# Attention beside a state-space scan on one core: two-bank ScalarE groups with an optional third bank, shared with VectorE

## The chip, the cores and the metric

The kernel runs on one core of one Trainium2 chip. The metric is the time of one execution in microseconds (us), as the device measures it. The program uses TensorE (PE), ScalarE (ACT), VectorE (DVE) and GpSimd (POOL), which work at the same time (busy for 93, 97, 87 and 57% of one span of 767.2 us in before) and which it makes wait for each other by semaphores, and a DMA queue (SP). Its matmuls write into PSUM, which it uses as eight banks of 128 x 512 fp32 numbers.

A run more than 1.5% above the fastest of its kernel counts as slow and is left out. A ratio below is the mean time of one kernel's fast runs over that of the other's fast runs of the same rounds, so it is not quite the ratio of the medians beside it. Brackets after a ratio are its 95% interval.

## The reference

Two independent layers, written side by side into one output.

```python
def _A_ref(x, Lambda_re, Lambda_im, B_re, B_im, C_re, C_im, log_dt, Dskip):   # x: 1 x 2048 x 640
    Lam_bar = jnp.exp(dt * Lam)                      # a complex diagonal state-space model
    Bu = jnp.einsum("bld,pd->blp", x + 0j, B_bar)
    for t in range(L):
        h = Lam_bar[None, :] * h + Bu[:, t, :]       # ... the scan over time
    return 2.0 * jnp.einsum("blp,dp->bld", hseq, Cmat).real + x * Dskip

def _B_ref(x, wq, wk, wv, wo):                       # 32 query heads of 20, one key and value head
    scores = jnp.einsum("bhqd,bkd->bhqk", q, k) * (Dh ** -0.5)
    p = _softmax(scores, axis=-1)                    # 32 x 2048 x 2048 exponentials
    o = jnp.einsum("bhqk,bkd->bhqd", p, v)
    return o.reshape(...) @ wo
# output: concatenate([a, b], axis=-1), bf16
```

The exponentials are what costs time. They are cut into 2048 tiles of 128 keys x 512 queries.

## The kernel before

The Python program is a planner. It keeps a list of operations with estimated durations, plays them through a simple model of the engines, and emits for each engine the order that the model chose. The order is fixed when the kernel is built.

A score tile goes one of two ways. *ScalarE tiles* are scored into a slot of several banks, and one ScalarE instruction exponentiates the whole slot into bf16 tiles "PR". *VectorE tiles* ("D" in the code) are scored into one bank, and VectorE makes an approximate exponential from integer arithmetic: one eviction "DR<-MB", then three shifted copies "DR<-DR", which VectorE or GpSimd make. The value matmuls then read PR or DR. PE, ScalarE and VectorE thus share 2048 tiles, and every tile that VectorE takes is one less for ScalarE.

```python
class Build:
    CHUNKS = (3, 2)     # two ScalarE slots: one of three banks, one of two
    MISC = 2            # two banks for VectorE score tiles and all other tasks; one more collects values
    NPS = 8             # eight exp buffers of three tiles each
    NDS = 18            # exp buffers of VectorE tiles
    SHARE = 0.25        # at most this share of tiles for VectorE
...
    def fill(self, op, i):                      # refill ScalarE slot i
        t, banks = self.slots[i]
        n = min(self.CHUNKS[i], NTILE - self.tile_n)
        h = self.hold[self.nhold % self.NPS]
        self.nhold += 1
        extra, used = [], set()
        while len(extra) < 4 - n and self.want_d(len(extra)):   # VectorE tiles scored beside it
            m = self.take_d(used)
            ...
            extra.append(m)
        tiles = [self.take_tile(used) for _ in range(n)]
        ...                                     # n score matmuls, then the extra ones
        dst = p.PR[:, h.index, 0:n, :]
        ex = self.act(lambda e: e.activation(dst, t[:, 0:512 * n], ACT.Exp, scale=1.0 / UNIT), ...)
...
    def want_d(self, taken=0):                  # may VectorE have another tile now?
        ...
        if len(self.d_banks()) <= taken:        # needs a free bank
            return False
        return len(self.d_free()) > taken + len(self.SHIFTS) - 1   # and free DR buffers
```

The state-space layer runs in the background as "tasks" in the misc banks: input matmuls (`xaT,BT` in the trace), a chain of VectorE rotations and scans, output matmuls (`CT`). PE also issues *filler* matmuls (`KT,VZ`) when the planner sees too little PE work in the last 3 us.

Of the kernel before, what the change touches and what calls it, by code (L numbers as in the profile page):

```python
# [9 lines left out]
ALU = mybir.AluOpType  # L10
AX = mybir.AxisListType
FP32 = mybir.dt.float32
BF16 = mybir.dt.bfloat16
# [26 lines left out]
class Schedule:  # L40
# [10 lines left out]
    SWITCH, STAY = 97.0, 1.2  # L51


    PAUSE = 1000.0
    LOCK = 60.0
    TABLE = 1280.0

# [329 lines left out]
class Holder:  # L387


    def __init__(self, index):  # L390
        self.index = index
        self.left = 0
        self.users = []
        self.taken = False
        self.waits = False


S, D, NC, H, DH = 2048, 640, 5, 32, 20
NQB, NKC, NGG = 4, 16, 8
# [5 lines left out]


class Build:
    CHUNKS = (3, 2)
    MISC = 2
    NPS = 8  # L410
    NOP = 7
    NRD = 3
    NDS = 18
# [16 lines left out]
    def build(self):  # L430
        nc = self.nc
        with ExitStack() as o:
            self.banks = []
            self.slots = []
            nb = 0
            for i, n in enumerate(self.CHUNKS):
                t = o.enter_context(nc.psum_tensor(f"SC{i}", [128, 512 * n], FP32))
                bs = [Bank(t, 512 * k, f"B{nb + k}") for k in range(n)]
                nb += n
                self.banks += bs  # L440
                self.slots.append((t, bs))
            rest = []
            for i in range(8 - nb):
                t = o.enter_context(nc.psum_tensor(f"MB{i}", [128, 512], FP32))
                rest.append(Bank(t, 0, f"B{nb + i}"))
            self.banks += rest
            self.pvbank = rest[-1]
            self.misc = rest[:self.MISC]
            self.early = [b for b in self.banks if b not in rest]
            self.alloc(o)  # L450
            base = nc.sbuf_bytes_remaining
            with ExitStack() as p1:
                self.alloc_early(p1)
                early = base - nc.sbuf_bytes_remaining
            with ExitStack() as p2:
                self.alloc_late(p2)
                late = base - nc.sbuf_bytes_remaining
                if late < early:
                    self.sb(p2, "pad", [128, (early - late) // 4 + 8], FP32)
                self.program()  # L460
                self.s.run()
                shares = {k: self.EARLY for k in self.LATE}
                shares.update({f"W{c}_1": [f"xbT{i}_{k}" for i in range(2) for k in range(NC)] for c in range(NC)})
                shares.update({f"CT{tb}_{c}": [f"xn{tb}"] for tb in range(2) for c in range(NC)})
                em = Emitter(nc, self.s.order, [b.key for b in self.banks], shares)
                em.plan()
                with nc.Block() as block:
                    em.emit(block)

    def alloc(self, o):  # L470
# [13 lines left out]
        self.VZ = sb(o, "VZ", [128, 32], BF16)  # L484
        self.WO = sb(o, "WO", [128, NC, 640], BF16)
        self.WOt = sb(o, "WOt", [128, 640], BF16)
        self.PR = sb(o, "PR", [128, self.NPS, max(self.CHUNKS), 512], BF16)
        self.tab = sb(o, "tab", [128, 2, NC, 512], BF16)
        self.Z = sb(o, "Z", [128, 2, NC, 512], BF16)
        self.prod = sb(o, "prod", [128, 4, 2, 512], BF16)  # L490
# [112 lines left out]
    def program(self):  # L603
# [7 lines left out]
        self.q_op, self.qd_op, self.half_op, self.scat_op, self.rd_op, self.brow_op = {}, {}, {}, {}, {}, {}  # L611
        self.o_ops, self.y_ops, self.w_op, self.xa_op = {}, {}, {}, {}
        self.state_op = {}
        self.hold = [Holder(i) for i in range(self.NPS)]
        self.nhold = 0
        self.dhold = [Holder(i) for i in range(self.NDS)]
        self.d_open = []
        self.d_left = collections.defaultdict(int)
# [24 lines left out]
    def warm_source(self):  # L643

        if self.started or self.s.t > 40000.0:
            return None
        p = self
        return Op("pe", [self.mm(self.pvbank.ap, p.PR[:, 0, 0, 0:128], p.PR[:, 0, 0, :], True, True)], 260.0, prio=9,
                  load=512.0, deps=[self.zero_op], reads=["PR0"], writes=[self.pvbank.key], hook=self.warm_last)


# [22 lines left out]
        self.pvbank.last = [op]  # L674

    def constants(self):
        self.zero_op = self.dve(lambda e: e.memset(self.PR[:, 0, 0, :], 0.0), 200, writes=["PR0"], prio=0.1)
        p = self
        self.c_op = {}

# [192 lines left out]
        self.give(bank)  # L873

    def take(self, which=None):
        for b in self.free_banks:
            if which is None or b in which:
                self.free_banks.remove(b)
                b.busy = True
                return b  # L880
        raise RuntimeError("no bank")
# [35 lines left out]
    def qt_task(self, bank):  # L917

        p = self
        prev = self.pe(self.four(bank, [p.VZ[:]] * 4, p.PR[:, 0, 0, :], True, False), self.mmt(512),  # L920
                       deps=[self.c_op["VZ"], self.zero_op] + bank.last, prio=0.95, mode="C", reads=["VZ", "PR0"], writes=[bank.key])
        for c in range(NC):
            prev = self.pe(self.four(bank, [p.wqf[:, 640 * c + 20 * j:640 * c + 20 * j + 20] for j in range(4)], p.xbT[:, c, 0:512],
# [108 lines left out]
    def attention(self):  # L1032
# [7 lines left out]
        fill = None  # L1040
        self.slot_last = [[op for b in bs for op in b.last] for _, bs in self.slots]
        self.pv_gate = list(self.pvbank.last)
        while self.tile_n < NTILE:
            i = k % len(self.slots)
            yield lambda: (fill is None or fill.start is not None) and all(o.start is not None
# [17 lines left out]

        for i in (k % 2, (k + 1) % 2):
            yield lambda: fill.start is not None and all(o.start is not None for o in self.slot_last[i])
            for bank in self.slots[i][1]:
                bank.last, bank.busy = list(self.slot_last[i]), False
                self.misc.append(bank)
                self.free_banks.append(bank)

    MARGIN = 650.0

# [21 lines left out]
    def fill(self, op, i):  # L1094
        p = self
        t, banks = self.slots[i]
        n = min(self.CHUNKS[i], NTILE - self.tile_n)
        h = self.hold[self.nhold % self.NPS]
        self.nhold += 1
        extra, used = [], set()  # L1100
        while len(extra) < 4 - n and self.want_d(len(extra)):
            m = self.take_d(used)
            if m is None:
                break
            extra.append(m)
        tiles = [self.take_tile(used) for _ in range(n)]
        ents = []
        for x, m in enumerate(tiles):
            b, kc, j = self.score(op, m, t[:, 512 * x:512 * x + 512], banks[x])
            ents.append((b, kc, j, p.PR[:, h.index, x, :]))  # L1110
        for m in extra:
            self.fill_d(op, m)
        op.reads = sorted(set(op.reads))
        op.dur = self.mmt(512, len(op.fns))
        op.load = 128.0 * len(op.fns)
        dst = p.PR[:, h.index, 0:n, :]
        ex = self.act(lambda e: e.activation(dst, t[:, 0:512 * n], ACT.Exp, scale=1.0 / UNIT),  # L1117
                      0.8333 * 512 * n + 64, table="exp",
                      deps=[op], reads=[b.key for b in banks[:n]], writes=[f"PR{h.index}"], prio=0.5,
                      gate=lambda: not h.taken or (h.left == 0 and self.s.done(h.users)))  # L1120

        def on_start(_):
            h.taken, h.left, h.users, h.waits = True, n, [], False
        h.waits = True
        ex.hook = on_start
        self.slot_last[i] = [ex]
        for b, kc, j, rhs in ents:
            self.pvq[b][j].append((p.VP[:, kc, 0:32], kc, rhs, f"PR{h.index}", ex, h, "VP"))
            self.pv_filled[b] += 1

    def score(self, op, m, out, bank):

# [65 lines left out]
    def want_d(self, taken=0):  # L1198
        s = self.s
        if self.tile_n >= NTILE - 8 or self.d_count + taken + 1 > self.SHARE * (self.tile_n - 16):  # L1200
            return False
        if len(self.d_banks()) <= taken:
            return False
        return len(self.d_free()) > taken + len(self.SHIFTS) - 1

# [27 lines left out]
        bank.last = [op]  # L1233
        self.give(bank)

    def fill_d(self, op, m):

        p = self
        bank = self.d_banks()[0]
        self.take([bank])  # L1240
        h = self.d_free()[0]
        self.d_count += 1
# [93 lines left out]
    def pv_source(self):  # L1336
# [16 lines left out]
            return None  # L1353
        complete = self.pv_filled[b] == 64 and not any(self.d_left[b, j] for j in range(4))
        left = sum(len(x) for x in q)
        h = self.hold[self.nhold % self.NPS]
        tight = h.taken and h.left > 0 or any(x.waits and x.left > 0 for x in self.hold)
        if len(group) < 4 and not tight and not (complete and left < 12 and len(group) == sum(1 for x in q if x)):
            return None
        prio = 0.9 if tight else self.PV  # L1360
        return Op("pe", [], self.mmt(512, len(group)), prio=prio, mode="C", load=128.0 * len(group), hook=lambda op: self.pv(op, b, group))

    def vp_seen(self, kc, t):
# [164 lines left out]
    def finish(self, prev, rows, bank, ops, end=None):  # L1528
# [3 lines left out]
        if end is None:  # L1532
            i = self.outs % 4
            self.outs += 1
            key, st = f"stg{i}", self.stg[:, i, :]
        else:
            key, st = f"PR{end}", self.PR[:, end, 0, :]
        last = self.stage_dma.get(key)
        if end in (4, 1, 3):
            ev = self.act(lambda e: e.activation(st, bank.ap, ACT.Copy), 600, deps=[prev], reads=[bank.key], writes=[key], prio=1)  # L1540
# [11 lines left out]
    def ssm_scalars(self):  # L1552
# [126 lines left out]
                               deps=self.ct_op[1], reads=[f"CT1_{c}" for c in range(NC)], writes=[f"CT1_{c}" for c in range(NC)], prio=3)  # L1679

        for c in range(NC):
            self.diag_op = self.dve(self.ts(p.diagD[:, c, :], p.ident[:], sc[:, DSK, c:c + 1], None, ALU.mult), 160,
                                    deps=[sc_op, self.c_op["ident"]], reads=["sc", "ident"], writes=["diagD"], prio=3)

    def unit_task(self, tb, c, ri, bank):
# [269 lines left out]
```

## Time and profile before

The median was 768.67 us (768.52 to 770.01, four runs).

| read from the profile of before | value |
|---|---|
| span of the profiled run | 767.2 us |
| ScalarE tiles / groups | 1604 / 642 |
| VectorE tiles | 444 |
| exponentials, merged busy time (overlaps counted once) | 726.7 us |
| idle of ScalarE just before exponentials | 5.7 us |
| first exponential starts / last one ends | 23.46 / 755.61 us |
| tail after the last exponential | 11.6 us |

From the page of before: the busy time of each engine, its share of the span and its instructions.

```profile
span 767.2 us, 24010 instructions
PE 716.6 (93%) x10217; PEld 239.1 (31%) x10217; DVE 666.2 (87%) x1239; ACT 743.2 (97%) x668; POOL 435.8 (57%) x454
```

The groups of instructions of before, each shape apart. The columns are line, engine, operation, output<-input, shapes, count, busy us and mean ns of one, then the idle time of the engine just before them and what ended it.

```profile
L1117 ACT ACTIVATE PR<-SC 128x1536 bf16<-128x1536 f32 x321 | 510.0, 1589 | 4.2 <-PE MB L585 2.5 <-PE SC L585 1.5
L600 DVE TENSOR_SCALAR DR<-MB 128x512 int16<-128x512 f32 x444 | 295.7, 684 | 64.2 <-PE MB L585 59.0 <-POOL DR L595 0.2
L1117 ACT ACTIVATE PR<-SC 128x1024 bf16<-128x1024 f32 x320 | 372.7, 1165 | 1.5 <-PE MB L585 1.4
```

The idle column is the one to read first. ScalarE never waits: 4.2 + 1.5 us before 641 exponentials. VectorE waits 64 us before its evictions, for PE to score something into a bank. So ScalarE is the limit, and VectorE has room but gets its tiles too late or too few. The mean durations (1589 and 1165 ns) overlap their neighbours, so their sum exceeds the time that they fill (510.0 + 372.7 us against 726.7 merged). The cost of a group has to be read from a stretch without gaps, as in this line of the windows of before for the tile PR (the second number under ACT is the count of exponentials):

```profile
core 0: us, PE busy (x) PEld busy (x) DVE busy (x) ACT busy (x), PEclk, DMA share, GB/s
510.00:657.00 147.00, 45.35 (x317) 11.58 (x317) 0.00 (x0) 147.00 (x131) 1.00 0.07 18
```

131 groups of 2.5 tiles on average in 147.0 us are 1.122 us each.

The timeline of ScalarE in before, merged; a bracket is idle time before the piece and what ended it. Gaps above a microsecond are rare.

```profile
23.46 4.62 ACT L1117 ACTIVATE PR<-SC 128x1536 bf16<-128x1536 f32 x4 [0.23 <-PE SC L585]
29.18 302.51 ACT L1117 ACTIVATE PR<-SC 128x1536 bf16<-128x1536 f32 x267 [1.10 <-PE SC L585]
333.06 68.82 ACT L1117 ACTIVATE PR<-SC 128x1024 bf16<-128x1024 f32 x61 [1.38 <-PE MB L585]
699.38 56.23 ACT L1117 ACTIVATE PR<-SC 128x1536 bf16<-128x1536 f32 x50 [1.91 <-PE MB L585]
```

### The profile page before, as it was taken

To read this page: it belongs to the slowest core of one execution; us is meant where nothing else is said; L and a number is where in the kernel's file an instruction comes from. 1 tells how busy PE (TensorE), PEld (TensorE's weight loads), DVE (VectorE), ACT (ScalarE), POOL (GpSimd) and SP (SyncE) were. 2 spreads that over 40 slices of the span, in tenths; PEclk is the share of its full clock that TensorE was granted. 3 is DMA by queue.
4 is the path that set the end of the run, shared out by engine and by line. 5 is a ranking of instruction groups with operands and counts; after the bars stand their busy time and mean duration, and the time that the engine had idled before them with its cause. 6 is when DMAs were issued, how large, how long until landed. Compare 5 with 4: busy or idle time off the path is not lost.

```text
span 767.2 us, 24010 instructions
## 1 busy us (share of the span) xinstructions
PE 716.6 (93%) x10217; PEld 239.1 (31%) x10217; DVE 666.2 (87%) x1239; ACT 743.2 (97%) x668; POOL 435.8 (57%) x454
## 2 busy tenths in 40 slices
PE   9999999998999999999889999999989999999997
PEld 3332223232223243332233322323322332233223
DVE  6989999898999888989899888998988889984786
ACT  5999999999999999999999999999999999999994
POOL 4765666466556544467635565446556556556961
PEclk9999999999999999999999999999999999999999
DMA  9934200100001111020001111120000110001001
GB/s 189 139 92 99 67 18 10 47 12 10 9 16 25 35 31 56 25 48 14 7 12 35 32 31 35 46 50 17 11 18 14 25 25 22 16 11 28 25 10 42
DMA packets 61770, 27.87 MB, mean 36 GB/s; under 512 B 44936, under 2 KB 61664, under 8 KB 61664
## 3 DMA queue, kind: packets, MB, share of 16 engines
q1 hardware_dynamic: 60332, 26.20, 14.7%
q8 instruction: 81, 1.33, 0.7%
q10 hardware_dynamic: 1332, 0.13, 0.2%
q14 instruction: 25, 0.20, 0.1%
HBM read 8.31 MB, written 8.12 MB: 21 GB/s over the span
## 4 chain that ended last, share of the span: by engine, by line
ACT 81%; PE 13%; DVE 3%; DMA 1%; SPq 1%; issue 0%; POOL 0%; ACTq 0%; DVEq 0%; POOLq 0%
ACT PR L1117 81%; PE MB L581 5%; PE MB L585 4%; PE SC L585 4%; DMA wqf<-in_B_wq_dram 1%; PE SC L581 1%; SPq L570 0%; DMA xaT<-in_A_x_dram 0%; DVE diagD L599 0%; DVE QP L956 0%; POOL fr L600 0%; DVE rot L1651 0%; DVE mab L814 0%; DVE prod L599 0%; DVE fr L600 0%
## 5 line engine op out<-in xcount | busy, mean ns | idle before, releaser
L1117 ACT ACTIVATE PR<-SC 128x1536 bf16<-128x1536 f32 (+1 forms) x642 | 726.7, 1376 | 5.7 <-PE MB L585 3.8
L595 POOL TENSOR_TENSOR DR<-DR,step 128x512 int32<-128x512 int32 x406 | 414.9, 1046 | 300.5 <-DVE DR L600 146.1
L600 DVE TENSOR_SCALAR DR<-MB 128x512 int16<-128x512 f32 x444 | 295.7, 684 | 64.2 <-PE MB L585 59.0
L585 PE MATMUL SC<-QT,KT 32*128 32x512 bf16 x1604 | 250.6, 385 | 40.0 <-ACT PR L1117 30.2
L585 PE MATMUL MB<-DR,VS 128*32 128x512 bf16 x1776 | 233.4, 385 | 0.4 <-DVE pvsb L1385 0.2
L585 PE MATMUL MB<-PR,VP 128*32 128x512 bf16 x1604 | 220.3, 385 | 0.9 <-DVE pvsb L1385 0.6
L585 PE MATMUL MB<-QT,KT 32*128 32x512 bf16 x444 | 160.4, 384 | 0.4 <-DVE prod L595 0.3
L585 PEld LDWEIGHTS SC<-QT,KT 32*128 32x128 bf16 x1604 | 63.9, 91 | 265.4 <-ACT PR L1117 179.8
L600 DVE TENSOR_SCALAR DR<-DR 128x1024 int16<-128x1024 int16 (+1 forms) x290 | 102.8, 408 | 7.9 <-PE MB L585 6.7
L585 PEld LDWEIGHTS MB<-DR,VS 128*32 128x32 bf16 x1776 | 59.5, 94 | 66.0 <-issue 38.1
L585 PEld LDWEIGHTS MB<-PR,VP 128*32 128x32 bf16 x1604 | 55.9, 94 | 63.2 <-issue 42.9
L581 PE MATMUL MB<-xaT,BT 128*32 128x512 bf16 x800 | 59.3, 383 | 0.4 <-DMA xaT<-in_A_x_dram 0.2
L595 DVE TENSOR_TENSOR prod<-MB,Z 128x1024 bf16<-128x1024 f32 x40 | 48.6, 1215 | 4.9 <-PE MB L581 4.4
L585 PE MATMUL MB<-KT,VZ 128*32 128x256 bf16 x876 | 48.5, 275 | 0.0
L585 PEld LDWEIGHTS MB<-QT,KT 32*128 32x128 bf16 x444 | 38.1, 91 | 24.1 <-issue 14.8
L1725 DVE TENSOR_TENSOR_SCAN g<-sc,hst,u 128x512 bf16<-128x512 f32 x30 | 39.6, 1327 | 0.0
L595 DVE TENSOR_TENSOR prod<-g,tab 128x1024 bf16<-128x1024 bf16 x40 | 31.4, 786 | 0.0
L581 PE MATMUL MB<-xbT,wqf 128*32 128x512 bf16 x400 | 29.6, 391 | 0.5 <-DVE DR L600 0.2
L581 PE MATMUL MB<-CT,W 128*32 128x512 bf16 (+1 forms) x640 | 29.4, 301 | 0.2 <-DVE DR L600 0.2
L581 PE MATMUL MB<-CT,xbT 128*32 128x512 bf16 (+1 forms) x640 | 28.5, 301 | 0.6 <-issue 0.4
L1542 DVE CAST stg<-MB 128x512 bf16<-128x512 f32 x35 | 24.0, 685 | 5.6 <-PE MB L581 5.3
L581 PE MATMUL MB<-WO,OP 128*32 128x128 bf16 (+1 forms) x580 | 27.1, 293 | 0.2
(137 smaller groups left out, 363.8 us busy)
## 6 DMA issues: line engine op xcount, KB each, us to landing
out_dram<-stg SPq DMA_DIRECT2D x35, 128.0 KB, 1.7
qd<-QP SPq DMA_DIRECT2D x20, 128.0 KB, 1.7
QT<-qd SPq DMA_DIRECT2D x28, 80.0 KB
OP<-pvsb SPq DMA_DIRECT2D x108, 20.0 KB
rdP<-recs SPq DMA_DIRECT2D x108, 20.0 KB
CT<-in_B_x_dram SPq DMA_DIRECT2D x2, 640.0 KB, 5.8
WO<-in_B_wo_dram SPq DMA_DIRECT2D x1, 800.0 KB, 4.7
wqf<-in_B_wq_dram SPq DMA_DIRECT2D x1, 700.0 KB, 6.1
```

Of the source, the lines that this page charges most:

```text
L581: r = e.matmul(out[32 * j:32 * j + 32], lhsT=lhsT[:, 32 * j:32 * j + 32], rhs=rhs, start=start, stop=stop, tile_position=(0, 32 * j), skip ...
L585: return lambda e: e.matmul(out, lhsT=lhsT, rhs=rhs, start=start, stop=stop, **kw)
L595: return lambda e: e.tensor_tensor(out, a, b, op)
L600: return lambda e: e.tensor_scalar(out, a, s1, s2, op0=op0, op1=op1)
L1117: ex = self.act(lambda e: e.activation(dst, t[:, 0:512 * n], ACT.Exp, scale=1.0 / UNIT), 0.8333 * 512 * n + 64, table="exp", deps=[op], re ...
L1542: ev = self.dve(lambda e: e.tensor_copy(st, bank.ap), 620, deps=[prev], reads=[bank.key], writes=[key], prio=self.EV, gate=(lambda: last.e ...
L1725: o = self.dve(lambda e, ri=ri, init=init: e.tensor_tensor_scan(p.g[:, u, ri, :], rdec, p.u[:, ri, :], init, ALU.mult, ALU.add), 1280, por ...
```

## The change

Intent: give VectorE and the tasks a third bank without taking it from ScalarE for good. Both slots now have three banks, but the third of each is a misc bank. A ScalarE group takes two banks, and the third as well if it is free when the slot is refilled and VectorE does not want it. The eight exp buffers of three tiles, of which two-tile groups would leave a third empty, become one ring of 24 single tiles. Four rules of the planner change along with it: VectorE gets no new tile while the state-space half is more than 120 tiles behind its plan (*pacing*); an overdue VectorE chain gains priority 500 instead of 1000 ns after the last one (*pause*); the last value matmuls of a block are hurried (*early closing*); one VectorE operation gets the planner's `port` mark, with which the planner does not let it overlap GpSimd operations that have the mark too (*port flag*).

```diff
-    PAUSE = 1000.0
+    PAUSE = 500.0
-    CHUNKS = (3, 2)
-    MISC = 2
-    NPS = 8
+    CHUNKS = (3, 3)
+    MISC = 1
+    NPT = 24
 ...
+        for _, bs in self.slots:              # the third banks join the misc banks
+            self.misc.append(bs[2])
+            self.free_banks.append(bs[2])
 ...
     def fill(self, op, i):
-        n = min(self.CHUNKS[i], NTILE - self.tile_n)
-        h = self.hold[self.nhold % self.NPS]
-        while len(extra) < 4 - n and self.want_d(len(extra)):
+        third = banks[2]
+        while len(extra) < 2 and self.want_d(len(extra)):
 ...
+        for m in extra:
+            self.fill_d(op, m, third)
+        n = min(2, NTILE - self.tile_n)
+        if n == 2 and len(extra) < 2 and self.tile_n < NTILE - 2 and third in self.d_banks():
+            n = 3
+            self.take([third])
         tiles = [self.take_tile(used) for _ in range(n)]
+        h = self.pr_take(n)                   # n neighbouring tiles of the ring
 ...
+    LAG = 120
+    def behind(self):                         # is the state-space half behind its plan?
 ...
-        if len(self.d_banks()) <= taken:
+        if len(self.d_banks()) <= taken or self.behind():
 ...
-        prio = 0.9 if tight else self.PV
+        prio = 0.9 if tight or complete else self.PV
 ...                                           # and port=True on the diagD operation
```

More of the change, by code (lines that the diff above doesn't have):

```diff
@@ L394, in __init__ @@
         self.taken = False
-        self.waits = False
+        self.prev = []
 S, D, NC, H, DH = 2048, 640, 5, 32, 20
@@ L446, in build @@
             self.banks += rest
-            self.pvbank = rest[-1]
+            self.pvbank, self.rest = rest[-1], rest
             self.misc = rest[:self.MISC]
@@ L486, in alloc @@
         self.WOt = sb(o, "WOt", [128, 640], BF16)
-        self.PR = sb(o, "PR", [128, self.NPS, max(self.CHUNKS), 512], BF16)
+        self.PR = sb(o, "PR", [128, self.NPT, 512], BF16)
         self.tab = sb(o, "tab", [128, 2, NC, 512], BF16)
@@ L613, in program @@
         self.state_op = {}
-        self.hold = [Holder(i) for i in range(self.NPS)]
-        self.nhold = 0
+        self.owner = [None] * self.NPT
+        self.pr_at = 0
+        self.waiting = []
         self.dhold = [Holder(i) for i in range(self.NDS)]
@@ L647, in warm_source @@
         p = self
-        return Op("pe", [self.mm(self.pvbank.ap, p.PR[:, 0, 0, 0:128], p.PR[:, 0, 0, :], True, True)], 260.0, prio=9,
+        return Op("pe", [self.mm(self.pvbank.ap, p.PR[:, 0, 0:128], p.PR[:, 0, :], True, True)], 260.0, prio=9,
                   load=512.0, deps=[self.zero_op], reads=["PR0"], writes=[self.pvbank.key], hook=self.warm_last)
@@ L676, in constants @@
     def constants(self):
-        self.zero_op = self.dve(lambda e: e.memset(self.PR[:, 0, 0, :], 0.0), 200, writes=["PR0"], prio=0.1)
+        self.zero_op = self.dve(lambda e: e.memset(self.PR[:, 0, :], 0.0), 200, writes=["PR0"], prio=0.1)
         p = self
@@ L875, in take @@
     def take(self, which=None):
-        for b in self.free_banks:
+        for b in sorted(self.free_banks, key=lambda b: b not in self.rest):
             if which is None or b in which:
@@ L919, in qt_task @@
         p = self
-        prev = self.pe(self.four(bank, [p.VZ[:]] * 4, p.PR[:, 0, 0, :], True, False), self.mmt(512),
+        prev = self.pe(self.four(bank, [p.VZ[:]] * 4, p.PR[:, 0, :], True, False), self.mmt(512),
                        deps=[self.c_op["VZ"], self.zero_op] + bank.last, prio=0.95, mode="C", reads=["VZ", "PR0"], writes=[bank.key])
@@ L1065, in attention @@
             yield lambda: fill.start is not None and all(o.start is not None for o in self.slot_last[i])
-            for bank in self.slots[i][1]:
+            for bank in self.slots[i][1][:2]:
                 bank.last, bank.busy = list(self.slot_last[i]), False
-                self.misc.append(bank)
-                self.free_banks.append(bank)
+                if bank not in self.misc:
+                    self.misc.append(bank)
+                    self.free_banks.append(bank)
     MARGIN = 650.0
@@ L1096, in fill @@
         t, banks = self.slots[i]
-        n = min(self.CHUNKS[i], NTILE - self.tile_n)
-        h = self.hold[self.nhold % self.NPS]
-        self.nhold += 1
+        third = banks[2]
         extra, used = [], set()
-        while len(extra) < 4 - n and self.want_d(len(extra)):
+        while len(extra) < 2 and self.want_d(len(extra)):
             m = self.take_d(used)
@@ L1105, in fill @@
             extra.append(m)
+        for m in extra:
[4 more added lines that the diff above has]
+            self.take([third])
         tiles = [self.take_tile(used) for _ in range(n)]
+        h = self.pr_take(n)
+        keys = [f"PR{h.index + x}" for x in range(n)]
         ents = []
@@ L1109, in fill @@
             b, kc, j = self.score(op, m, t[:, 512 * x:512 * x + 512], banks[x])
-            ents.append((b, kc, j, p.PR[:, h.index, x, :]))
-        for m in extra:
-            self.fill_d(op, m)
+            ents.append((b, kc, j, p.PR[:, h.index + x, :]))
         op.reads = sorted(set(op.reads))
@@ L1115, in fill, with pr_take, pr_next, tight @@
         op.load = 128.0 * len(op.fns)
-        dst = p.PR[:, h.index, 0:n, :]
+        dst = p.PR[:, h.index:h.index + n, :]
         ex = self.act(lambda e: e.activation(dst, t[:, 0:512 * n], ACT.Exp, scale=1.0 / UNIT),
                       0.8333 * 512 * n + 64, table="exp",
-                      deps=[op], reads=[b.key for b in banks[:n]], writes=[f"PR{h.index}"], prio=0.5,
-                      gate=lambda: not h.taken or (h.left == 0 and self.s.done(h.users)))
+                      deps=[op], reads=[b.key for b in banks[:n]], writes=keys, prio=0.5,
+                      gate=lambda: all(x.taken and x.left == 0 and self.s.done(x.users) for x in h.prev))
         def on_start(_):
-            h.taken, h.left, h.users, h.waits = True, n, [], False
-        h.waits = True
+            h.taken, h.left, h.prev = True, n, []
+            self.waiting.remove(h)
+        self.waiting.append(h)
         ex.hook = on_start
         self.slot_last[i] = [ex]
-        for b, kc, j, rhs in ents:
-            self.pvq[b][j].append((p.VP[:, kc, 0:32], kc, rhs, f"PR{h.index}", ex, h, "VP"))
+        if n == 3:
+            self.s.spawn(self.d_give(third, ex))
+        for (b, kc, j, rhs), key in zip(ents, keys):
+            self.pvq[b][j].append((p.VP[:, kc, 0:32], kc, rhs, key, ex, h, "VP"))
             self.pv_filled[b] += 1
+    def pr_take(self, n):
+        at = self.pr_next(n)
+        h = Holder(at)
+        for x in self.owner[at:at + n]:
+            if x is not None and x not in h.prev:
+                h.prev.append(x)
+        self.owner[at:at + n] = [h] * n
+        self.pr_at = at + n
+        return h
+    def pr_next(self, n):
+        return self.pr_at if self.pr_at + n <= self.NPT else 0
+    def tight(self):
+        at = self.pr_next(3)
+        return any(x is not None and x.taken and x.left for x in self.owner[at:at + 3]) \
+            or any(x.left for h in self.waiting for x in h.prev)
+    LAG = 120
+    def behind(self):
+        while self.next_unit < NQB * NC:
+            w = self.w_op.get(divmod(self.next_unit, NC))
+            if w is None or w.start is None:
+                return self.tile_n > self.unit_due[divmod(self.next_unit, NC)] + self.LAG
+            self.next_unit += 1
+        return False
+    next_unit = 0
     def score(self, op, m, out, bank):
@@ L1234, in d_give, with fill_d @@
         self.give(bank)
-    def fill_d(self, op, m):
+    def fill_d(self, op, m, own=None):
         p = self
-        bank = self.d_banks()[0]
+        bank = min(self.d_banks(), key=lambda b: (b is own, b.key))
         self.take([bank])
@@ L1355, in pv_source @@
         left = sum(len(x) for x in q)
-        h = self.hold[self.nhold % self.NPS]
-        tight = h.taken and h.left > 0 or any(x.waits and x.left > 0 for x in self.hold)
+        tight = self.tight()
         if len(group) < 4 and not tight and not (complete and left < 12 and len(group) == sum(1 for x in q if x)):
             return None
-        prio = 0.9 if tight else self.PV
+        prio = 0.9 if tight or complete else self.PV
         return Op("pe", [], self.mmt(512, len(group)), prio=prio, mode="C", load=128.0 * len(group), hook=lambda op: self.pv(op, b, group))
@@ L1536, in finish @@
         else:
-            key, st = f"PR{end}", self.PR[:, end, 0, :]
+            key, st = f"PR{3 * end}", self.PR[:, 3 * end, :]
         last = self.stage_dma.get(key)
@@ L1681, in ssm_scalars @@
         for c in range(NC):
-            self.diag_op = self.dve(self.ts(p.diagD[:, c, :], p.ident[:], sc[:, DSK, c:c + 1], None, ALU.mult), 160,
+            self.diag_op = self.dve(self.ts(p.diagD[:, c, :], p.ident[:], sc[:, DSK, c:c + 1], None, ALU.mult), 160, port=True,
                                     deps=[sc_op, self.c_op["ident"]], reads=["sc", "ident"], writes=["diagD"], prio=3)
```

## The prediction

> **What bounds the kernel now.** ScalarE. The engine summary has it busy 743.2 of 767.2 us; the chain of waits puts 81% of the span on its exponentials. The groups of instructions show 642 exponentials, 726.7 us busy, with only 5.7 us of idle time before them in total. They run from 23.5 us (start of the first) to about 755.6 us; the rest is a head of 23.5 us and a tail of 11.6 us (output projection of the last block, eviction, store). PE looks full at 93%, but its waits show about 210 us spent waiting for an exponential to free its score banks, so PE has slack. VectorE, at 87%, has about 100 us idle, 64 us of it before score evictions, waiting for PE.
>
> **Cost of one exponential.** The timeline between 510 and 657 us shows 131 back to back groups (3 and 2 banks in turn, 2.5 tiles each) in 147.0 us: 1.122 us per group. The chain's stretch of 54 groups took 61.13 us, 1.132 each. [...] the trace decides, I use 0.065.
>
> **What changes.** From the two compiled orders:
> - Exponential groups: 321 of three banks + 320 of two + 1 of one become 195 + 503 + 1. ScalarE tiles fall from 1604 to 1592 (VectorE takes 456 instead of 444). ScalarE saves 12 x 0.427 = 5.1 us and pays 57 x 0.065 = 3.7 us: net -1.4 us, all on the critical path.
> - VectorE: 12 more evictions at 0.684 us, plus copies: about +12 us with 100 idle. Off the path.
> - PE: stretches of score matmuls rise from 654 to 670[...]; value-matmul groups are nearly unchanged (1396 to 1405 quads). [...] fewer filler matmuls (876 to 708).
> - Waits: a two-bank group runs about 0.92 us, a three-bank one 1.35. Before, the two alternated, so only every second refill had the short window. Now five in seven do, in runs of up to 19. And the third bank is shared with VectorE's score tiles and with tasks, so a late VectorE eviction can now hold back a ScalarE group. I expect idle time before exponentials to go from 5.7 to about 8 us.
> - Ring of 24 tiles: exponentials hardly ever wait for their buffers now, so worth nearly nothing.
> - Head and tail: nearly the same order; within 1 us.
>
> **Prediction.** -1.4 + 2.3 = about +1: 769.5 us, range 763 to 777. Chances: faster by over 2% 0.02, within 2% 0.92, slower 0.06. A large gain is impossible: 1592 tiles are 679 us of elements, plus 45 us of fixed cost, plus 35 us of head and tail.
>
> **What would show each step right.** In the groups of instructions: about 503 two-bank and 195 three-bank exponentials, merged busy time near 725 us. Idle before them 5 to 12 us, released by PE score matmuls. VectorE busy time near 678 us.  First exponential at 23 to 25 us; last ends 11 to 12 us before the end of the span.
>
> **What would make it wrong.** If VectorE falls behind its plan, PE, which works in order, would wait for a bank and the next short group would starve ScalarE: tens of us of idle before exponentials, time above 777. If the fixed cost of a two-bank group is larger than 0.065 us, say 0.12, another 3 us come on top. If the idle time vanishes and the tail shortens, 764 us is possible.

The sum reads -1.4 us of ScalarE's work and +2.3 us of idle time, about +1 on 768.67, so 769.5 us.

- 0.427 us a tile: the two shapes of before differ by one tile, and their means by 0.424 us (1589 less 1165 ns); the fit below has 0.426. With 0.427 the groups of 2.5 tiles, 1.122 and 1.132 us each, leave the 0.055 and 0.065 us a group. The 0.92 and 1.35 us of a two-bank and a three-bank group are estimates from 0.427 and 0.065; kernel 3 shows 694.33 us for 756 two-bank groups, 0.918 each.
- PE's busy time went from 716.6 to 716.4 us.

## The result

| | before | changed |
|---|---|---|
| median of the first comparison, us | 768.67 (768.52 to 770.01) | 766.74 (766.19 to 767.15) |
| ratio of the fast runs | 1 | 0.9971 [0.9953, 0.9988] |
| profiled span, us | 767.2 | 764.4 |
| ScalarE tiles / groups | 1604 / 642 | 1592 / 699 |
| exponentials, busy us | 726.7 | 724.7 |
| idle before exponentials, us | 5.7 | 5.2 |
| first exponential starts, us | 23.46 | 23.52 |
| last exponential ends, us | 755.61 | 753.45 |
| tail, us | 11.6 | 10.9 |

The profiled span fell by 2.8 us. The stretch of exponentials gives 2.2 of it (732.15 to 729.93), nearly all from their busy time, and the tail 0.6.

From the page of the changed kernel:

```profile
span 764.4 us, 23858 instructions
PE 716.4 (94%) x10083; PEld 230.4 (30%) x10084; DVE 668.5 (87%) x1266; ACT 741.0 (97%) x725; POOL 442.2 (58%) x457
```

The groups of instructions of the changed kernel, each shape apart:

```profile
L1126 ACT ACTIVATE PR<-SC 128x1024 bf16<-128x1024 f32 x503 | 480.9, 1169 | 2.4 <-PE SC L585 2.0 <-PE MB L585 0.3
L1126 ACT ACTIVATE PR<-SC 128x1536 bf16<-128x1536 f32 x195 | 279.5, 1604 | 2.8 <-PE SC L585 2.7
L600 DVE TENSOR_SCALAR DR<-SC 128x512 int16<-128x512 f32 x366 | 243.4, 683 | 42.4 <-PE SC L585 40.5 <-PE MB L585 0.4
L600 DVE TENSOR_SCALAR DR<-MB 128x512 int16<-128x512 f32 x90 | 61.4, 682 | 10.2 <-PE SC L585 7.4 <-PE MB L585 2.0
```

VectorE evicts 366 + 90 = 456 tiles, 366 of them from third banks (SC). Its idle time before evictions fell from 64.2 to 52.6 us. That is the intended effect, and it is small: 12 tiles. ScalarE pays for it with 57 more groups.

The timeline of ScalarE in the changed kernel:

```profile
29.10 19.76 ACT L1126 ACTIVATE PR<-SC 128x1536 bf16<-128x1536 f32 x17 [1.40 <-PE SC L585]
50.83 6.09 ACT L1126 ACTIVATE PR<-SC 128x1024 bf16<-128x1024 f32 x6 [1.98 <-PE SC L585]
60.78 255.10 ACT L1126 ACTIVATE PR<-SC 128x1536 bf16<-128x1536 f32 x244 [1.13 <-PE SC L585]
316.03 322.07 ACT L1126 ACTIVATE PR<-SC 128x1024 bf16<-128x1024 f32 x314 [0.15 <-PE MB L585]
638.26 115.19 ACT L1126 ACTIVATE PR<-SC 128x1024 bf16<-128x1024 f32 x112 [0.15 <-PE MB L585]
```

From 61 us on there is no gap worth a name, although most refills now have the short time window of a two-bank group. Nearly all idle time lies between 27 and 61 us; before had its first gap, 1.10 us, at the same place as the changed kernel's 1.40 us, where the clock of both was low (0.50 for 3.41 us, from 24.95 us in before and from 26.61 us in the changed kernel). From 54 us on the windows of the changed kernel show the granted TensorE clock (PEclk, third number from the end, as a share of full speed) falling to half:

```profile
core 0: us, PE busy (x) PEld busy (x) DVE busy (x) ACT busy (x) POOL busy (x), PEclk, DMA share, GB/s
48.00:51.00 3.00, 2.46 (x39) 0.56 (x31) 2.54 (x4) 1.02 (x2) 1.87 (x2) 1.00 0.13 38
51.00:54.00 3.00, 1.93 (x16) 0.59 (x15) 3.00 (x8) 3.00 (x4) 0.92 (x1) 0.99 0.29 79
54.00:57.00 3.00, 3.00 (x18) 0.53 (x16) 2.63 (x5) 2.92 (x3) 2.98 (x4) 0.50 0.13 45
57.00:60.00 3.00, 3.00 (x30) 0.69 (x27) 0.94 (x3) 2.48 (x2) 1.94 (x3) 0.50 0.09 22
60.00:63.00 3.00, 3.00 (x42) 0.87 (x38) 1.91 (x4) 2.22 (x2) 1.55 (x3) 0.88 0.34 74
```

The 1.98 us gap comes first (48.85 to 50.83 us, ScalarE waiting for scores), then a stretch with little PE work, then about six microseconds at half clock, in which PE is busy without pause and ScalarE starves for another 1.13 us. Before had full clock over this time, and ScalarE was never idle (same columns):

```profile
51.00:54.00 3.00, 2.38 (x37) 0.89 (x38) 2.88 (x6) 3.00 (x4) 1.67 (x2) 1.00 0.41 101
54.00:57.00 3.00, 2.70 (x40) 1.11 (x41) 2.74 (x5) 3.00 (x4) 2.73 (x4) 1.00 0.13 31
```

### The profile page after: what moved, and what is told of

Read it like the earlier page. It is cut to its first block, busy times and chain, and to the rows that moved or that the text cites. A ratio compares the mean times of both kernels' runs of the same rounds, so it can differ in the third digit from the quotient of the medians.

```text
span 764.4 us, 23858 instructions
## 1 busy us (share of the span) xinstructions
PE 716.4 (94%) x10083; PEld 230.4 (30%) x10084; DVE 668.5 (87%) x1266; ACT 741.0 (97%) x725; POOL 442.2 (58%) x457
## 4 chain that ended last, share of the span: by engine, by line
ACT 88%; PE 10%; DVE 2%; POOL 0%; issue 0%; DVEq 0%; POOLq 0%
ACT PR L1126 87%; PE MB L585 4%; PE SC L585 3%; PE MB L581 2%; PE SC L581 1%; DVE QP L957 0%; DVE DR L600 0%; ACT tab L1666 0%; POOL fr L600 0%; DVE fr L600 0%; DVE prod L599 0%; ACT L1672 0%; DVE Z L1714 0%; ACT PR L1584 0%; DVE mab L815 0%
## 5 line engine op out<-in xcount | busy, mean ns | idle before, releaser
L1126 ACT ACTIVATE PR<-SC 128x1024 bf16<-128x1024 f32 (+1 forms) x699 | 724.7, 1290 | 5.2 <-PE SC L585 4.7
L585 PE MATMUL SC<-QT,KT 32*128 32x512 bf16 x1958 | 283.5, 386 | 33.6 <-ACT PR L1126 26.5
L600 DVE TENSOR_SCALAR DR<-SC 128x512 int16<-128x512 f32 x366 | 243.4, 683 | 42.4 <-PE SC L585 40.5
L600 DVE TENSOR_SCALAR DR<-DR 128x1024 int16<-128x1024 int16 (+1 forms) x305 | 111.7, 416 | 12.1 <-PE MB L585 8.8
L600 DVE TENSOR_SCALAR DR<-MB 128x512 int16<-128x512 f32 x90 | 61.4, 682 | 10.2 <-PE SC L585 7.4
L581 PE MATMUL MB<-xaT,BT 128*32 128x512 bf16 x660 | 50.0, 383 | 0.1
L595 DVE TENSOR_TENSOR prod<-MB,Z 128x1024 bf16<-128x1024 f32 x33 | 40.1, 1216 | 5.7 <-PE MB L581 5.5
L585 PE MATMUL MB<-KT,VZ 128*32 128x256 bf16 x708 | 39.5, 275 | 0.0
L585 PE MATMUL MB<-QT,KT 32*128 32x512 bf16 x90 | 34.8, 387 | 4.4 <-ACT PR L1126 3.2
L581 PE MATMUL MB<-CT,W 128*32 128x128 bf16 (+1 forms) x600 | 27.7, 296 | 0.1
```

Source lines behind the costliest of these rows:

```text
L581: r = e.matmul(out[32 * j:32 * j + 32], lhsT=lhsT[:, 32 * j:32 * j + 32], rhs=rhs, start=start, stop=stop, tile_position=(0, 32 * j), skip ...
L585: return lambda e: e.matmul(out, lhsT=lhsT, rhs=rhs, start=start, stop=stop, **kw)
L595: return lambda e: e.tensor_tensor(out, a, b, op)
L600: return lambda e: e.tensor_scalar(out, a, s1, s2, op0=op0, op1=op1)
```

## The experiments

All kernels of the experiments gave correct results. Tile and group counts quoted in the expectations were counted in the compiled orders, not timed. The first theory, **A**: the time follows a sum, ScalarE's tiles and groups at a fixed cost each plus a constant head and tail; the banks matter only by how many tiles they move to VectorE. Rivals: the ring frees ScalarE (**R**), the new rules do it (**S**), a group costs nothing extra (**G**), the short refill windows starve ScalarE (**W**).

The first four kernels also make a square of layout against rules.

### 1. The ring alone

Edit, against the changed kernel: the old bank layout and the old rules back, the ring kept.

```diff
-    CHUNKS = (3, 3)
-    MISC = 1
+    CHUNKS = (3, 2)
+    MISC = 2
-        while len(extra) < 2 and self.want_d(len(extra)):
+        n = min(self.CHUNKS[i], NTILE - self.tile_n)
+        while len(extra) < 4 - n and self.want_d(len(extra)):
 # the optional third bank goes, and with it the four rules:
 # PAUSE = 1000, no behind(), no "or complete", no port flag
```

> The old bank layout (groups of 3 and 2 in turn, two banks for VectorE) and the old rules of the planner, with the ring of 24 exp tiles only. Its compiled order has 1608 ScalarE tiles in 643 groups (before: 1604 in 642). Sum rule: 0.427 us a tile and 0.065 us a group give +1.8 us on before, about 770.5 us. Theory A (the gain is ScalarE's tiles and groups; the ring only stores): 769.5 to 771.5, idle before exponentials unchanged at 4 to 7 us. Rival R (the ring is what frees ScalarE): at or under the changed kernel, 767 or less, idle under 3 us.

Measured: 770.71 us, ratio 1.0019 [1.0007, 1.0031]; exponentials busy 728.2 us, idle before them 5.2 us. As A expected; the ring by itself buys nothing. The planner simply made a slightly different plan with four more ScalarE tiles. R is out in the old layout; the new layout without the ring was not run.

### 2. The rules alone

Edit: as in 1, but the four new rules stay.

> The old bank layout with the ring and the new rules (pacing of the state-space half, 500 ns pause, early closing of a block, port flag). 1611 ScalarE tiles in 645 groups: +3.2 us on before by the sum rule. Theory A: about 771.5 us (770 to 773), slower than before. Rival S (the new rules made the gain by a better order and a shorter tail, the banks are neutral): 766 to 768, tail under 11 us.

Measured: 772.18 us, ratio 1.0043 [1.0031, 1.0055]; exponentials busy 730.5 us, idle 5.7 us, tail 11.5 us. As A expected, and S is out: in the old layout the new rules bring no gain. Whether they cost anything there is not shown, because three VectorE tiles fewer than in kernel 1 are within what replanning alone moves (see the end). The profile of this kernel also has the clock at 0.50 to 0.77 between 53 and 62 us, with the old banks.

### 3. Groups of two only

Edit, against the changed kernel:

```diff
-        if n == 2 and len(extra) < 2 and self.tile_n < NTILE - 2 and third in self.d_banks():
+        if n == 2 and len(extra) < 2 and self.tile_n < NTILE - 2 and third in self.d_banks() and False:
```

> The changed kernel, but a ScalarE group never takes the third bank: 795 groups of two, 1590 tiles. Tiles are as few as in the changed kernel, 96 groups more. Theory A with a fixed cost of 0.065 us a group: 96 x 0.065 - 2 x 0.427 = +5.4 us on the changed kernel, about 772 us, exponentials busy about 730 us, idle before them about the same (4 to 8 us). Rival G (fixed cost hidden in the overlap, a group costs nothing): 766. Rival W (short refill windows starve ScalarE): idle before exponentials over 15 us and more than 780.

Measured: 778.31 us (774.00 to 780.99), ratio 1.0114 [1.0092, 1.0136]. The group of exponentials in its profile:

```profile
L1126 ACT ACTIVATE PR<-SC 128x1024 bf16<-128x1024 f32 x795 | 731.2, 1128 | 10.3 <-PE SC L585 9.7
```

Busy time came out as A said (731.2 against 730). Against the changed kernel it has 2 tiles fewer and 96 groups more and is 6.5 us longer: (6.5 + 2 x 0.426) / 96 = 0.077 us a group. G is out. The total was missed by 6 us: idle doubled to 10.3 us. 8 of the 10.3 us lie in one stretch: a gap of 4.38 us that ended at 53.8 us, at full clock, and then 0.5 to 0.9 us before each of several groups up to 70 us, while the granted clock was 0.5 to 0.6. W is out at full clock. In the large gap PE had 52 filler matmuls in its order and then waited 0.91 us for a VectorE operation of the state-space half, with the scores behind it. And from 70.4 us to the last one, 756 groups, all with the short window, ran as one piece:

```profile
70.40 694.33 ACT L1126 ACTIVATE PR<-SC 128x1024 bf16<-128x1024 f32 x756 [0.93 <-PE SC L585]
```

At the low clock the gaps are real, but kernel 2, whose groups of 3 and 2 alternate, has them too (1.7 us between 55 and 62 us), so they are not shown to come from the short windows. Five of its six runs had a mean clock of 0.985 to 0.990; the one at 0.997 took 774.00 us, 2 us above A's figure.

### 4. The layout alone

Edit, against the changed kernel: the four rules back to the old ones.

```diff
-    PAUSE = 500.0
+    PAUSE = 1000.0
-        if len(self.d_banks()) <= taken or self.behind():
+        if len(self.d_banks()) <= taken:
-        prio = 0.9 if tight or complete else self.PV
+        prio = 0.9 if tight else self.PV
 # and no port flag on diagD
```

> The new banks and the ring under the old rules (no pacing, pause 1000 ns, no early closing, no port flag). 1574 ScalarE tiles in 703 groups: by the sum rule ScalarE is 7.4 us shorter than in the changed kernel. But in its compiled order 80 of the 800 input matmuls and 320 of the 1280 output matmuls of the state-space half come after the last score matmul (none in before and after). Theory P (pacing is needed: VectorE takes the freed banks for score tiles and the state-space half falls behind): the last exponential ends near 746 us, but the tail after it grows from 11 us to 30 us or more, total 775 to 790. Rival L (the rules are a brake, the banks alone are better): total 758 to 761.

Measured: 789.64 us, ratio 1.0276 [1.0259, 1.0292]. ScalarE indeed had less to do: exponentials busy 718.4 us, the last one ending at 747.37 us. But the tail was 39.5 us. Its ScalarE timeline ends with the first line, and VectorE's timeline then shows what the end waits for:

```profile
734.43 12.94 ACT L1126 ACTIVATE PR<-SC 128x1024 bf16<-128x1024 f32 x14 [0.40 <-PE MB L585]
```

```profile
756.42 1.27 DVE L1769 TENSOR_TENSOR_SCAN g<-sc,hst,u 128x512 bf16<-128x512 f32 x1
761.06 1.28 DVE L1769 TENSOR_TENSOR_SCAN g<-sc,hst,u 128x512 bf16<-128x512 f32 x1
764.30 2.45 DVE L1769 TENSOR_TENSOR_SCAN g<-sc,hst,u 128x512 bf16<-128x512 f32 x2
772.99 0.69 DVE L1586 CAST stg<-MB 128x512 bf16<-128x512 f32 x1 [4.14 <-PE MB L581]
782.67 0.69 DVE L1586 CAST stg<-SC 128x512 bf16<-128x512 f32 x1 [1.69 <-PE SC L581]
```

These are scans and output tiles of the state-space half, run alone at the end of the kernel. P's mechanism is right: VectorE took the new bank for score tiles (474 instead of 456), and its other duty fell behind. Which of the rules prevents it, kernels 5 and 6 ask.

The square, as ratios to before:

| | old rules | new rules |
|---|---|---|
| old layout (with ring) | 1.0019 | 1.0043 |
| new layout | 1.0276 | 0.9971 |

The layout alone makes the kernel 2.8% slower, and the rules alone gain nothing. Only both together gain, 0.3%.

**The sum.** A least-squares fit to the busy times of exponentials in six kernels (before, changed, 1 to 4) gives 0.426 us a tile and 0.067 us a group, with no residual over 0.8 us. In the seven other plans that follow it is off by 1.2 us at most (kernel 11; with the unrounded 0.4261 and 0.0674).

### 5. Without pacing

Edit, against the changed kernel: only `or self.behind()` taken out.

> The changed kernel with only the pacing rule taken out (the 500 ns pause stays). 1585 ScalarE tiles in 706 groups: with 0.426 us a tile and 0.067 us a group, fitted to the busy times of six kernels so far, exponentials are busy 722 us, 2.5 us less than in the changed kernel. In its compiled order no state-space matmul comes after the last score matmul. Theory P1 (pacing alone is what kept the state-space half in time): tail over 20 us, total over 775. Theory P2 (the shorter pause suffices; pacing costs score tiles of VectorE): tail 10 to 13 us, total 763 to 766.

Measured: 769.70 us (766.81 to 773.23), ratio 1.0000 [0.9978, 1.0021]. In the profile, of a 766.81 us run, exponentials were busy 722.8 us and the tail was 11.7 us. So P1 is out: with the shorter pause the state-space half is in time without pacing. But P2's total was missed too. Idle before exponentials was 7.6 us, and the six runs spread over 6 us in step with their mean granted clock, from 766.81 us at 0.992 to 773.23 us at 0.979. This is the second effect, outside the sum. The fewer ScalarE tiles are real, and in the profiled run, the fastest of the six, they are lost again to idle time and tail.

### 6. Without pacing and with the old pause

Edit, against the changed kernel: `or self.behind()` out and `PAUSE = 1000.0`.

> The changed kernel without pacing and with the old pause of 1000 ns; early closing and the port flag stay. 1578 ScalarE tiles in 705 groups (719 us busy). 40 input and 320 output matmuls of the state-space half come after the last score matmul. Theory P2 (without pacing it is the shorter pause that keeps the state-space half in time): tail 25 to 40 us, total 776 to 790. Rival (early closing or the port flag does it): tail under 15 us, total 766 or less.

Measured: 783.76 us, ratio 1.0197 [1.0181, 1.0214]; exponentials busy 719.9 us, the last one ending at 751.55 us, tail 33.1 us. Together with 5: without pacing it is the pause that decides (tail 11.7 or 33.1 us), not the early closing or the port flag, which both kernels have. The fourth corner, pacing with the old pause, was compiled but not run; its order has the 456 VectorE tiles of the changed kernel and no state-space work after the last score matmul either, so pacing may suffice by itself.

### 7 and 8. More VectorE exp buffers, in both layouts

Edit, in the changed kernel and in before: `NDS = 18` becomes `NDS = 20`.

> The changed kernel with 20 instead of 18 VectorE exp buffers. 1582 ScalarE tiles in 698 groups, 466 VectorE tiles. Theory A: exponentials busy 721 us, 4 us less than in the changed kernel; total 761 to 764. Rival (VectorE at 87% is full, more of its tiles make PE wait): idle before exponentials over 10 us, total 766 or more.

> The kernel before with 20 instead of 18 VectorE exp buffers. 1603 ScalarE tiles in 641 groups, 445 VectorE tiles (before: 444). Theory B (with two misc banks it is the banks that limit VectorE's tiles, so buffers buy nothing there, while with three they do): same time as before within 1 us, 768 to 770. Rival (buffers help in both layouts): 766 or less.

Measured: the changed kernel with 20 buffers 764.88 us, ratio to before 0.9933 [0.9921, 0.9946], exponentials busy 721.5 us, idle 7.8 us. Before with 20 buffers 770.86 us, ratio 1.0010 [0.9998, 1.0022], busy 726.0 us. With two misc banks buffers buy nothing, with three they buy ten VectorE tiles. So the third bank did move the limit, from banks to buffers, and the change as made stopped at the next limit. Here A's total was missed by 1 us: 2.6 us of the 3.2 us gained in busy time came back as idle in the profiled run.

### 9. Buffers traded for ring

Edit, against the changed kernel: the ring shrinks to pay for VectorE buffers, and three planner constants move. They were picked by planning a few hundred variants without running them.

```diff
-    NPT = 24
+    NPT = 21
-    NDS = 18
+    NDS = 22
-    MARGIN = 650.0
+    MARGIN = 600.0
-    ... GRACE = 90, 1780, 20, 40
+    ... GRACE = 90, 1780, 20, 20
-    PAUSE = 500.0
+    PAUSE = 750.0
```

> The changed kernel with 22 VectorE exp buffers, a ring of 21 exp tiles in their place, and three constants of the planner moved (margin 600, grace 20, pause 750). 1577 ScalarE tiles in 688 groups, 471 VectorE tiles; no state-space work after the last score matmul. Theory A: exponentials busy 718 us, 7 us less than in the changed kernel, total 757 to 762. Rival (VectorE full): idle before exponentials over 10 us, total 765 or more.

Measured: 764.12 us (762.55 to 764.75), ratio 0.9923 [0.9911, 0.9934]; exponentials busy 718.5 us as the sum says, idle 6.5 us, but a tail of 13.7 us. It beats both kernels. A's total was missed by 2 us, by the longer tail.

### 10. The changed kernel again

> The changed kernel once more, as a control on the chip of these runs: 0.995 to 0.999 of before, mean TensorE clock 0.993 to 0.995 with a dip between 50 and 62 us.

Measured, on another chip: five fast runs of 765.20 to 772.39 us with clocks of 0.987 to 0.995, ratio 0.9979 [0.9953, 1.0006]. One run, the profiled one, took 886.29 us at a mean clock of 0.655, with 0.62 to 0.65 in every 10 us from 10 to 790 us, as far as it was read; it is a slow run and is left out. Over the nine fast runs of both comparisons the time follows the mean clock closely (correlation -0.93). The 33 runs of before in the experiments span 768.21 to 770.88 us at 0.995 to 0.998. So the changed kernel is faster by about 2 us in the median of either comparison, by 4 us in its two runs at 0.995 here, and slower by 3 us in the run at 0.987: it is less steady. The expected clock, 0.993 to 0.995, was missed by three of the five fast runs, and the dip could not be looked for, since the profiled run was the slow one.

### 11. More filler

Theory **C**, an assumption from the changed kernel's windows (PE busy 1.93 of 3 us, then a clock of 0.50): too little PE work in a stretch lowers the clock. The changed kernel has 708 filler matmuls where before has 876. Edit, against the changed kernel: `KEEP = 3500.0` becomes `KEEP = 4400.0`.

> The changed kernel with the planner's threshold for filler matmuls raised from 3500 to 4400: 1296 filler matmuls instead of 708. 1583 ScalarE tiles in 700 groups. The changed kernel's profile has a TensorE clock of 0.5 from 54 to 60 us, after a stretch in which PE was nearly idle, and 1.1 us of idle before an exponential at its end. Theory C (too little PE work in a window lowers the clock, filler prevents it): mean clock 0.996 or more in most runs, spread of the runs under 1.5 us, exponentials busy 721.5 us, idle before them 4 us or less, total 761 to 763. Rival (the filler takes PE time that the score refills need): idle before exponentials over 8 us, total 766 or more.

Measured: 770.27 us (767.72 to 773.42), ratio 1.0013 [0.9993, 1.0032]; mean clocks 0.985 to 0.994; exponentials busy 722.9 us, idle 13.3 us. C's remedy failed: nearly twice the filler did not keep the clock up. ("Nearly idle" in the expectation is too strong: PE was busy 1.93 of 3 us.) The new filler did not close the gap either: from 52.3 to 55.7 us PE was busy 58% of the time, and the clock fell to half at its end. The windows show dips at 20 to 40, 50 to 70, 130 to 140 and 380 to 390 us. The idle time went up as the rival said, but with the clock down as well the run can't tell which of the two did it.

### 12. Buffers, ring of 18 and a little filler

Edit, against the changed kernel: `NPT = 18`, `NDS = 24`, `KEEP = 3800.0`, `MARGIN = 700.0`, GRACE 20, `PAUSE = 750.0`.

> The changed kernel with 24 VectorE exp buffers, a ring of 18 exp tiles in their place, filler threshold 3800, margin 700, grace 20, pause 750. 1577 ScalarE tiles in 697 groups, 900 filler matmuls. Exponentials busy 719 us by the sum rule. Theories A and C: clock 0.995 or more, idle before exponentials under 6 us, total 758 to 761, under the 764 of the tuned kernel without more filler. Rival (a ring of 18 is too short, or the clock dips all the same): idle over 8 us, 763 or more.

Measured: 763.48 us (761.42 to 764.95), ratio 0.9924 [0.9911, 0.9938]; busy 718.5 us, idle 7.0 us, clocks 0.990 to 0.997. Busy time as the sum says, but A's total was missed by 2.5 us: idle stayed at 7 us, and the tail was 12.9 us. The same time as kernel 9 within the intervals. The run at 0.997 was the fastest of all runs, 761.42 us.

## Why the prediction was right or wrong

- **Total.** Predicted 769.5 us (763 to 777), measured 766.74. The class, within 2%, was right, and the sign of the central figure was wrong: +1 predicted, -2 measured. The range, 14 us, is seven times the effect, so that it holds the total says little.
- **ScalarE's sum.** Predicted -1.4 us from 12 tiles fewer at 0.427 us and 57 groups more at 0.065 us; measured -2.0 us in busy time. Six kernels confirm the sum (0.426 and 0.067), so the mechanism was right. The remaining 0.6 us is of the size of the fit's residuals.
- **Idle before exponentials.** This is the term that was mis-sized: "from 5.7 to about 8 us" predicted, 5.2 measured. With the sum's -2.0 us and the tail's -0.6 us it turns +1 into -2. The reason given, that five in seven refills now have the short window, did not show from 61 us on, where the refills kept up, nor in the 756 short windows in a row of kernel 3. What idle time there is lies in the early stretch with gaps and a low clock, which the prediction did not name; that 5.2 us lies inside its expected 5 to 12 us is luck.
- **VectorE.** Predicted +12 us of busy time; the page shows +2.3 us (666.2 to 668.5), although the evictions alone grew by 9.1 us in their own sum (295.7 to 243.4 + 61.4) and the copies by 8.9 us (102.8 to 111.7). Where the rest was saved was not taken apart. It is off the path in both.
- **Ring worth nearly nothing.** Right in the old layout, by experiment 1; not tested in the new one.
- **Head and tail within 1 us.** Right: +0.06 and -0.6 us.
- **What it did not see.** The rules in the diff entered only through the counts of the compiled order; none was weighed. They are half of the change: without them the same banks lose 2.8% (experiment 4). The prediction did name VectorE falling behind as its risk, but with the wrong path: it expected starved ScalarE groups, and what came was a tail of 39.5 us, with 5.8 us of idle before exponentials. And it didn't see that the TensorE clock could dip in the new order.

The clock dip at 53 to 62 us goes with the shorter pause, not with the new banks. In the profiled runs it is there in all eight kernels with a pause of 500 or 750 ns, kernel 2 with the old banks among them, and in none of the five with 1000 ns, kernel 4 with the new banks among them. Kernels 5 and 6 differ in the pause alone; the first line is of 5, the second of 6 (columns as in the windows above):

```profile
50.00:60.00 10.00, 8.79 (x84) 2.20 (x76) 8.32 (x16) 8.63 (x9) 6.06 (x6) 0.83 0.19 52
50.00:60.00 10.00, 8.10 (x97) 2.40 (x93) 8.36 (x16) 8.01 (x9) 6.79 (x7) 1.00 0.17 49
```

Little PE work often went before a fall. In the traces of before and of the changed kernel the clock changes lie whole multiples of 3.41 us apart (in the changed kernel the first stretches are 20.48, 3.41, 23.89 and 6.83 us). Cut along that grid, by the author's count, the thirteen fast profiles have 2721 steps at full clock between 31 and 755 us, and the clock fell after 14 of them. The eight steps in which PE was busy least (52 to 61%) were all followed by a fall. In the changed kernel the step before the fall, 50.50 to 53.91 us, had 69%. But the busy share does not decide alone: the other six falls came after 66 to 85%, and ring-alone's step of 74% at 51.4 us, kernel 6's of 76% at 54.8 us and before's of 67% at 557.4 us and 69% at 332.2 us had none. PE work was not varied with all else held, so this is a count and not an experiment.

What stays open is how the shorter pause makes the stretch with little PE work, and why the first gap, at 48.85 us, arises. In the trace PE, which is bound to its order, waits there for a GpSimd copy (0.41 us) ahead of the score matmuls, but that is only a part of the gap.

A further point on the size of the gain. Replanning both kernels under small changes of planner constants, without running them, gave 434 to 444 VectorE tiles for before and 455 to 462 for the changed kernel. Before as it stood (444) was at the top of its range and the changed kernel (456) near the bottom of its own. That part of the comparison is only counted; experiments 1 and 2 are two such plans of the old layout that were run, at 440 and 437 tiles.

## What to carry to other kernels

When one engine is saturated, count what the change makes it do (elements and instructions) before anything else: here two coefficients explained the exponentials' busy time of thirteen plans within 1.2 us of some 720. Giving an idle engine more of the shared work helped here only while its other duties kept their place (kernel 4 had a tail of 39.5 us); look for work left after the last instruction of the bottleneck. And after moving one limit, ask for the next: with the third bank in place two more buffers brought another 0.4%, somewhat more than the 0.2 to 0.3% of the change itself, while without it they brought nothing.
